# A fused linear-attention and gated-MLP kernel: the order of its steps searched anew under changed plan constants

## The chip, the core and the metric

The kernel runs on one core of one Trainium2 chip. The metric is the device time of one execution in microseconds (us), the median of several runs. The engines of the core are TensorE (PE in the profile, with its weight loads as PEld), VectorE (DVE), ScalarE (ACT), GpSimd (POOL) and SyncE (SP, which here only issues DMAs).

## What is computed

A quadratic-feature linear attention over 4 batches, 4 heads, 1088 positions and head dimension 32, followed by an RMS norm and a gated MLP (SiLU) over all 4352 positions with model width 128 and inner width 1536. All inputs are 32-bit floats.

```python
def phi(x):                       # 8 x 8 products = 64 features
    a = einsum('rd,bhsd->bhsr', S1, x)
    b = einsum('rd,bhsd->bhsr', S2, x)
    return einsum('bhsi,bhsj->bhsij', a, b).reshape(..., 64)
q_p, k_p = phi(q), phi(k)
kv  = einsum('bhsf,bhsd->bhfd', k_p, v)
num = einsum('bhsf,bhfd->bhsd', q_p, kv)
den = einsum('bhsf,bhf->bhs', q_p, sum(k_p over s)) + 1e-06
x   = (num / den) as [4352, 128]
xn  = x / sqrt(mean(x * x) + 1e-06) * rms_g
out = (silu(xn @ w_gate) * (xn @ w_val)) @ w_out
```

## The kernel before

The work falls into *steps* (the class Task). There are 1254 of them, numbered in the order in which the program adds them, and each carries the instructions of one piece of work on one engine:

- the key side of a batch (kside): loads of the keys kt and the values vt, the projection of the keys into PSUM (L519 for batch 0, L497 for the others), a copy both, the outer product phi, and the product with the values into kv (L531), which is copied into SBUF (steps 30 and 31 for batch 0, the tiles kv,0,0 and kv,0,1);
- the query side of a chunk (qside) of 512 positions (the ninth has 256): a load of q, its projection (L594 for chunks 0 and 1, L622 for the others), the outer product phiq, turned by PE for chunks 0 and 1 (L602) or spread through DRAM for the others (far, at, bt), the product with kv (L678), the division (den, rden, x), the squares ms, the inverse root rstd on POOL, the scaling xn, a transpose of xn (L758 for the first two chunks, through DRAM for the others) and the rounding into x_hi and x_lo;
- the weights: a load w_raw of 384 KB for each twelfth of the inner width, its head w_top, the joined w_full, the rounded w_hi and the remainder w_lo;
- the slots (slot): for each chunk c and each twelfth j three matmuls for the gate (g_ps, L802), three for the value (v_ps, L802), SiLU on ACT (s, L811), the product h on DVE (L814), its rounding h_hi and remainder h_lo (L832), and three matmuls into o_ps (L840). The three matmuls stand for one product of higher accuracy: high by high, low by high and high by low parts.

Nothing of the order is left to chance. The list ORDER gives the sequence of all 1254 steps, and the string ON gives, for the 354 steps that have a choice, the engine (a for ACT, d for DVE, p for POOL). Each engine works through its own steps in the sequence of the list, and the DMA issues of SP stand in the same list. The function follow walks along the list and works out, with constants for durations, semaphore hops, DMA flight and instruction fetches, when each step would start. Two things on the chip come of it: the sequence of emission (by planned start, which along one engine is the sequence in the list), and the fillers. Where the plan sees PE idle before EARLY (7 us), or idle for more than GAP behind it, it puts in matmuls on zeros that nobody reads (keep_warm, L382). The first seven of these stand there in any case.

Steps and lines that the argument follows: step 14 (g_ps from the first keys, L519) and step 18 (v_ps from the same piece of keys, L519); steps 32 and 37 (the two halves of query chunk 0, L594); step 428 (query chunk 3, L622, 16 matmuls); steps 56 and 61 (the transposes of the two halves of x of chunk 0, L758); step 66 (w_top of weight 0 on ACT, L401); steps 36 and 41 (phiq of chunk 0); steps 55 and 60 (the scaling xn of the two halves on ACT, L731), 57 (x_hi of the first half on ACT, L764); steps 186 and 190 (the first L802 matmuls of slot 1).

The starting parts of the plan's DMA model, the part of follow that the change touches:

```python
begin = max(wire, at + FLIGHT + OTHER * (w.since > 0))
wire = begin + w.lat
while fetches and fetches[0] < wire:
    wire += FETCH_WIRE * (begin < fetches.pop(0) + FETCH_WIRE)
t.end = wire + SETTLE + (w.occ - ISSUE if w.since else 0)
if len(landed) < len(LAGS):
    t.end += LAGS[len(landed)]
```

Of the kernel before, what the change touches and what calls it, by code (L numbers as in the profile page):

```python
# [39 lines left out]
LAGS = (210, 240, 740)  # L40
# [13 lines left out]
1 0 2 6 9 3 14 10 15 4 32 33 7 37 16 5 64 34 18 38 19 12 26 27 22 20 146 39 28 147 11 23 24 151 35 40 41 65 17 13 148 21 25 36 29 152 153 149 66 72  # L54
67 30 73 31 74 68 42 48 43 44 150 45 49 69 50 75 154 46 155 47 54 243 244 427 246 51 52 132 131 245 156 8 53 157 158 162 163 159 55 428 135 77 164
161 165 136 429 84 56 59 60 137 57 79 61 76 190 58 228 85 173 186 229 160 177 187 62 188 86 178 191 87 174 63 166 551 189 192 80 167 175 248 176 168
179 180 194 134 88 430 94 193 81 206 232 169 181 82 89 170 171 83 138 199 250 195 182 140 200 133 172 70 78 99 201 207 247 208 433 288 249 71 202 183
234 209 233 302 289 304 303 142 104 95 96 281 90 114 100 552 196 139 141 184 290 91 92 143 434 197 210 185 305 105 93 106 306 97 282 125 307 291 257
213 198 283 231 98 284 295 203 296 214 204 211 292 285 293 255 297 309 251 215 252 298 115 205 216 107 553 101 116 253 217 221 108 145 102 311 218
220 119 286 256 212 222 223 310 117 331 224 316 333 312 144 332 126 254 225 318 103 554 120 219 109 334 317 319 299 226 325 227 368 287 127 129 324  # L60
118 370 258 300 320 259 265 121 294 301 308 130 326 123 313 314 327 260 261 369 346 412 110 111 124 335 371 345 315 321 322 266 347 413 267 262 268
239 269 112 431 432 270 235 348 435 263 328 264 352 440 329 354 323 372 113 439 359 441 271 353 336 375 377 416 418 272 376 436 338 355 330 337 417
373 273 340 675 230 339 437 378 341 389 391 237 442 360 676 438 236 238 678 240 677 443 923 449 396 349 350 356 361 241 277 342 362 397 275 343 274
344 357 382 398 242 363 364 399 404 276 278 403 279 390 280 405 351 358 392 384 406 556 400 365 465 366 444 450 445 446 487 401 451 393 374 383 452
557 394 385 486 379 380 467 479 466 488 448 381 558 489 500 555 386 563 501 481 468 480 387 454 388 395 482 502 682 559 565 564 680 566 469 407 483
415 560 402 561 453 447 493 473 408 679 490 455 503 562 456 484 457 414 472 474 475 470 409 410 924 926 573 567 574 419 460 514 458 575 515 495 568
521 569 476 799 516 517 494 504 528 471 477 496 570 530 491 529 522 576 505 577 478 485 461 523 524 531 459 462 572 578 681 1047 684 497 411 542 532
535 498 544 463 537 492 533 571 518 579 536 525 499 538 507 464 508 589 509 590 526 510 511 591 592 580 519 603 543 605 581 512 545 604 596 624 606
506 513 520 527 534 925 598 626 685 689 625 546 582 610 539 421 540 597 627 688 585 541 547 683 686 617 593 584 612 611 607 608 583 586 587 599 631
619 613 594 618 548 645 549 633 687 690 632 800 802 801 804 620 420 929 422 697 423 691 424 639 600 601 805 614 634 635 636 659 660 661 662 595 588  # L70
692 602 647 646 806 621 638 693 615 609 698 648 652 699 654 426 653 616 628 640 622 649 629 650 425 666 655 727 641 623 729 656 694 642 803 643 721
728 730 668 720 722 657 700 630 702 667 755 695 723 713 715 637 928 813 812 696 811 701 814 669 809 670 644 651 663 671 703 704 714 930 757 734 664
756 550 758 807 658 748 665 735 716 724 808 810 705 717 709 736 784 1048 1049 725 737 750 738 731 128 707 718 739 1050 815 816 817 821 818 822 783
1052 672 742 741 673 706 708 785 732 786 759 743 719 726 760 749 733 744 710 776 823 777 1051 751 778 790 745 711 762 779 763 791 712 746 824 1053
752 792 793 769 740 764 753 927 936 837 747 931 826 771 754 780 765 770 839 761 825 367 766 767 820 893 794 935 838 819 827 795 844 772 840 894 933
773 781 768 895 1054 774 846 896 828 932 934 937 829 865 787 845 847 788 938 841 859 851 867 775 897 898 866 853 868 872 782 842 858 860 848 789 849
869 852 796 854 830 797 900 870 873 843 833 861 880 831 832 834 862 874 875 902 855 856 879 1059 881 1060 914 850 857 863 864 876 1061 882 901 1057
1055 886 1056 916 1062 945 883 939 884 1058 903 946 1063 887 798 947 888 877 948 835 674 836 1064 889 915 890 871 878 917 950 949 968 970 907 891 918
1065 909 908 885 989 910 969 971 961 963 940 941 942 919 904 943 962 911 964 944 951 905 892 899 991 1066 912 965 996 990 992 993 975 952 953 954 998
906 913 977 976 1067 1068 1069 1070 972 994 997 1003 920 978 982 973 983 999 966 921 984 979 980 1005 1004 957 967 1006 1010 1012 985 1038 1000 956  # L80
1040 974 122 1011 1013 1017 1024 986 1039 1001 1018 981 1026 1041 1042 1032 987 988 1007 1008 1019 1020 995 1002 955 958 959 1031 1043 960 1009 1033
1014 1034 1107 1129 1021 1071 1022 1073 1108 1109 1110 1015 1111 1079 1075 1128 1130 1131 1074 1081 1025 1027 1028 1016 1023 1029 1035 1036 1086 1088
1087 1093 1089 1094 1095 1096 1072 1076 1030 1077 1142 1097 1090 1091 1080 1082 1037 1044 1144 1045 1143 1101 1083 1100 1102 1084 1098 1085 1121 1145
1114 1116 1103 1104 1105 1146 1046 1078 1122 1092 1147 1123 1124 1115 1099 1135 1117 1118 1112 1149 1132 1137 1136 1106 922 1150 1133 1151 1172 1138
1152 1139 1113 1125 1174 1156 1119 1157 1179 1173 1158 1126 1165 1120 1127 1175 1140 1167 1153 1159 1154 1180 1181 1182 1134 1141 1160 1193 1187 1166
1161 1186 1168 1176 1195 1148 1200 1169 1188 1155 1177 1201 1189 1183 1184 1170 1194 1196 1214 1162 1202 1229 1203 1216 1197 1228 1163 1215 1207 1164
1190 1198 1230 1171 1178 1191 1185 1231 1243 1209 1217 1208 1218 1222 1245 1221 1232 1219 1210 1192 1199 1204 1205 1206 1223 1236 1233 1224 1211 1225
1212 1237 1226 1244 1213 1238 1246 1220 1227 1234 1240 1242 1247 1239 1249 1235 1251 1241 1253 1248 1250 1252
"""
ON = (  # L90
# [17 lines left out]
SWITCH = 138  # L108
RING, ISSUE, FAR, FLIGHT, SETTLE, RATE = 8, 470, 640, 900, 1300, 380
OTHER = 300  # L110
AHEAD, FETCHED, BLOCK, ASK, FETCH = 62, 210, 128, 2600, 2400
STALL = (3200, 0)
FETCH_WIRE, FETCH_AT = 1300, (9800, 16300, 26400, 31000)
COLD = (5600, 1.5)
# [35 lines left out]
class Plan:  # L150
# [32 lines left out]
    def follow(self, clock0, filler):  # L183
# [7 lines left out]
        for i in map(int, ORDER.split()):  # L191
            t = self.tasks[i]
            e = t.on
            w = t.ways[e]
# [757 lines left out]
```

## Time and profile before

| | us |
| --- | --- |
| median of three runs | 252.21 |
| lowest and highest run | 252.2, 252.3 |
| the profiled execution, time | 252.34 |
| the profiled execution, span from the first to the last instruction | 250.4 |
| PE busy in the span | 246.5 |
| DVE busy | 180.6 |
| ACT busy | 132.8 |
| POOL busy | 81.9 |

The profiled execution is one run of the program with the hardware profiler. Its span goes from the first instruction to the last; its time has some 2 us more around it. PE's instructions are pipelined, and their ends are modelled, so neighbouring rows overlap: the distance from start to start is the cost of one. The idle time in brackets behind a row is that of its engine just before it.

### The profile page before, as it was taken

What the parts mean: (1) busy time and instruction counts of PE and PEld (TensorE: products, weight loads), DVE (VectorE), ACT (ScalarE), POOL (GpSimd) and SP (SyncE); (2) the same over time, 40 slices, a digit from 0 to 9 for tenths busy, and PEclk for the clock granted to TensorE, in tenths of its full rate; (3) what the DMA queues carried; (4) which work ended last, traced back from release to release, by engine and by line L of the source; (5) the groups of instructions that cost most, each with busy time, mean ns of one, the idle gap of its engine ahead of it and who ended that gap; (6) DMA issues with size and microseconds to landing.
All of it is one profiled execution on the core that took longest, in us unless ns stands there. A gap on an engine that the chain in (4) does not pass through costs nothing.

```text
span 250.4 us, 5878 instructions
## 1 busy us (share of the span) xinstructions
PE 246.5 (98%) x2244; PEld 198.7 (79%) x2244; DVE 180.6 (72%) x410; ACT 132.8 (53%) x287; POOL 81.9 (33%) x80
## 2 busy tenths in 40 slices
PE   8999999999999999999999999999999999999995
PEld 5977788777888788878888788888888888888894
DVE  1899998789467887575587678855678576765672
ACT  3686988564444747353445643553356464355351
POOL 4447031343664223223550403265332203132201
PEclk9999999999999999999999999999999999999999
DMA  6989892552371332321610254251002102010010
GB/s 238 359 265 343 269 251 91 158 152 45 108 205 41 86 98 77 105 86 34 183 34 1 47 153 112 45 149 61 3 0 46 41 3 43 21 63 3 0 42 21
DMA packets 19691, 25.55 MB, mean 102 GB/s; under 512 B 3152, under 2 KB 11472, under 8 KB 19664
## 3 DMA queue, kind: packets, MB, share of 16 engines
q1 hardware_dynamic: 19232, 24.54, 33.3%
q10 hardware_dynamic: 432, 0.66, 0.7%
q8 instruction: 17, 0.28, 0.4%
q14 instruction: 10, 0.08, 0.1%
HBM read 20.40 MB, written 4.78 MB: 101 GB/s over the span
## 4 chain that ended last, share of the span: by engine, by line
PE 98%; DVE 0%; issue 0%
PE v_ps L802 29%; PE g_ps L802 29%; PE o_ps L840 28%; PE att L678 3%; PE att L531 2%; PE o_ps L382 2%; PE att L622 1%; PE o_ps L531 1%; PE att L594 1%; PE att L758 1%; PE att L497 1%; PE g_ps L678 0%; PE att L602 0%; PE v_ps L678 0%; PE att L821 0%; PE g_ps L519 0%
## 5 line engine op out<-in xcount | busy, mean ns | idle before, releaser
L811 ACT ACTIVATE s<-g_ps 128x512 f32<-128x512 f32 (+1 forms) x108 | 61.0, 574 | 71.4 <-PE g_ps L802 38.1
L814 DVE TENSOR_TENSOR h<-v_ps,s 128x512 f32<-128x512 f32 (+2 forms) x110 | 69.8, 647 | 40.0 <-PE v_ps L802 27.7
L832 POOL TENSOR_TENSOR h_lo<-h,h_hi 128x512 fp32r<-128x512 f32 (+1 forms) x42 | 52.9, 1267 | 104.5 <-DVE h_lo L832 43.9
L350 ACT CAST h_hi<-h 128x512 fp32r<-128x512 f32 (+1 forms) x70 | 41.3, 601 | 19.9 <-DVE h L814 17.4
L832 DVE TENSOR_TENSOR h_lo<-h,h_hi 128x512 fp32r<-128x512 f32 (+1 forms) x64 | 41.4, 652 | 5.5 <-ACT h_hi L350 3.6
L802 PE MATMUL v_ps<-x_hi,w_hi 128*128 128x512 f32 (+1 forms) x110 | 41.9, 381 | 0.0
L802 PE MATMUL g_ps<-x_hi,w_hi 128*128 128x512 f32 (+1 forms) x110 | 41.9, 381 | 0.0
L802 PE MATMUL v_ps<-x_hi,w_lo 128*128 128x512 f32 (+1 forms) x110 | 41.6, 378 | 0.0
L802 PE MATMUL g_ps<-x_hi,w_lo 128*128 128x512 f32 (+1 forms) x110 | 41.5, 378 | 0.0
L802 PE MATMUL g_ps<-x_lo,w_hi 128*128 128x512 f32 (+1 forms) x110 | 41.5, 379 | 0.0
L802 PE MATMUL v_ps<-x_lo,w_hi 128*128 128x512 f32 (+1 forms) x110 | 41.3, 378 | 0.0
L840 PE MATMUL o_ps<-h_hi,w_hi 128*128 128x512 f32 (+1 forms) x106 | 40.9, 386 | 0.0
L840 PE MATMUL o_ps<-h_hi,w_lo 128*128 128x512 f32 (+1 forms) x106 | 40.8, 385 | 0.0
L840 PE MATMUL o_ps<-h_lo,w_hi 128*128 128x512 f32 (+1 forms) x106 | 40.8, 385 | 0.0
L802 PEld LDWEIGHTS v_ps<-x_hi,w_hi 128*128 128x128 f32 x110 | 20.6, 188 | 5.0 <-DVE w_lo L436 0.5
L802 PEld LDWEIGHTS g_ps<-x_hi,w_hi 128*128 128x128 f32 x110 | 20.7, 188 | 4.6
L802 PEld LDWEIGHTS v_ps<-x_hi,w_lo 128*128 128x128 f32 x110 | 20.7, 188 | 4.3
L802 PEld LDWEIGHTS g_ps<-x_hi,w_lo 128*128 128x128 f32 x110 | 20.7, 188 | 4.3
L802 PEld LDWEIGHTS g_ps<-x_lo,w_hi 128*128 128x128 f32 x110 | 20.6, 188 | 4.2
L802 PEld LDWEIGHTS v_ps<-x_lo,w_hi 128*128 128x128 f32 x110 | 20.5, 188 | 4.1
L840 PEld LDWEIGHTS o_ps<-h_lo,w_hi 128*128 128x128 f32 x106 | 19.9, 188 | 4.4
L840 PEld LDWEIGHTS o_ps<-h_hi,w_hi 128*128 128x128 f32 x106 | 19.9, 188 | 4.2
(112 smaller groups left out, 246.9 us busy)
## 6 DMA issues: line engine op xcount, KB each, us to landing
w_raw<-w SPq DMA_DIRECT2D x12, 384.0 KB
bt<-far SPq DMA_DIRECT2D x24, 128.0 KB
at<-far SPq DMA_DIRECT2D x12, 256.0 KB
outT<-o_sb SPq DMA_DIRECT2D x16, 128.0 KB
q<-qT SPq DMA_DIRECT2D x7, 256.0 KB
turned<-xq SPq DMA_DIRECT2D x24, 64.0 KB
xt<-turned SPq DMA_DIRECT2D x6, 256.0 KB
vt<-v SPq DMA_DIRECT2D x4, 272.0 KB
```

The source lines that it names most:

```text
L350: "act": on_act(n, lambda: nc.scalar.copy(out=out(), in_=in_()), True),
L382: nc.tensor.matmul(out=warm[:1, :cols], lhsT=zeros[:, :1], rhs=zeros[:, :cols], start=True, stop=True)
L497: nc.tensor.matmul(out=pair[p]()[a * D:(a + 1) * D, :g], lhsT=sblk[p * HALF:(p + 1) * HALF, p * NB // 2:(p + 1) * NB // 2], rhs=kt()[p * H ...
L531: nc.tensor.matmul(out=kvv[r0:r0 + wide, h // 2, :], lhsT=phi()[:, t, h * F + f:h * F + f + wide], rhs=vt()[:, t, h, :], start=(t == 0 and ...
L594: nc.tensor.matmul(out=ab()[hf * HALF:(hf + 1) * HALF, t * HALF:(t + 1) * HALF], lhsT=q()[:, s1:s1 + HALF], rhs=sblk, start=True, stop=True,)
L622: nc.tensor.matmul(out=accs[p]()[a * D:(a + 1) * D, :m], lhsT=sab[rows, p].rearrange("p c o r -> p (c o r)"), rhs=q()[rows, a * m:(a + 1) ...
L678: nc.tensor.matmul(out=nv[n0:n0 + wide, t, p, :], lhsT=phi()[:, p, l0:l0 + wide], rhs=kvs[(s0 + l0) // S][:, p, :], start=True, stop=True,)
L802: nc.tensor.matmul(out=acc()[:, cs], lhsT=wt[:, j, i3, :], rhs=x()[:, cs], start=(i == 0), stop=(i == 2))
L811: act(n, lambda: nc.scalar.activation(out=s()[:, :n], in_=gps()[:, :n], func=AF.Silu), cols(gps, whole[0]), [s])
L814: cs.stop - cs.start, lambda cs=cs: nc.vector.tensor_tensor(out=h()[:, cs], in0=vps()[:, cs], in1=s()[:, cs], op=ALU.mult),
L832: eng.tensor_tensor(out=h_lo()[:, :n], in0=h()[:, :n], in1=h_hi().bitcast(F32)[:, :n], op=ALU.subtract)
L840: nc.tensor.matmul(out=o_ps()[:, :n], lhsT=wt[:, j, 2, :], rhs=x()[:, :n], start=first and i == 0, stop=last and i == 2,)
```

## The change

Five constants of the plan take other values (the lags of the first loads, ASK, FETCH, FETCH_WIRE and FETCH_AT), one is added (LATE, which the plan adds to the beginning of every load), and the list ORDER and the string ON are replaced by the outcome of a new search under these constants. No step is added, removed or altered. Of the lists the first two lines stand here.

```diff
@@ -37,7 +37,7 @@
 STEP, EARLY = 107, 7000
-LAGS = (210, 240, 740)
+LAGS = (120, 240, 700)
 NATURAL = 2
...
 ORDER = """
-1 0 2 6 9 3 14 10 15 4 32 33 7 37 16 5 64 34 18 38 19 12 26 27 22 20 146 39 28 147 11 23 24 151 35 40 41 65 17 13 148 21 25 36 29 152 153 149 66 72
-67 30 73 31 74 68 42 48 43 44 150 45 49 69 50 75 154 46 155 47 54 243 244 427 246 51 52 132 131 245 156 8 53 157 158 162 163 159 55 428 135 77 164
...
+0 6 1 2 3 14 15 18 19 16 20 9 10 7 32 64 37 33 38 22 34 26 27 151 28 39 146 13 11 23 8 147 35 152 40 41 12 65 72 24 148 153 66 67 5 73 243 131 17 21
+25 29 149 31 36 30 42 154 74 150 75 76 43 427 132 44 77 45 46 4 84 155 48 49 156 68 47 162 50 51 157 52 158 54 53 59 244 135 79 55 159 163 164 70 246
...
 """
 ON = (
-    "dapapadaddaadaadddaaaaapapdapapaadaadaadaapaadaadaadaadaddaadppddaapaadaaddadadadadadadadpdddaadddaaapapadadapapaadapapd"
...
+    "ddddpddapadadaadadaaaaapapddpapaadaadaapaadaadaapaadaadaadaappppaadpaadaaadadadadadddadapddddaaddadaadadadapapddaadaddda"
...
 )
@@ -108,9 +108,10 @@
 OTHER = 300
-AHEAD, FETCHED, BLOCK, ASK, FETCH = 62, 210, 128, 2600, 2400
+AHEAD, FETCHED, BLOCK, ASK, FETCH = 62, 210, 128, 3300, 2800
+LATE = 150
 STALL = (3200, 0)
-FETCH_WIRE, FETCH_AT = 1300, (9800, 16300, 26400, 31000)
+FETCH_WIRE, FETCH_AT = 1100, (9750, 15200, 24500, 32000)
@@ -234,7 +235,7 @@
             if e == "dma":
-                begin = max(wire, at + FLIGHT + OTHER * (w.since > 0))
+                begin = max(wire, at + FLIGHT + LATE + OTHER * (w.since > 0))
                 wire = begin + w.lat
```

Counted along both lists: 393 steps are on PE in both. ACT has 265 steps before and 261 after, DVE 375 and 381, POOL 66 and 64, and DMA 155 in both. 25 h_lo go from POOL to DVE and 18 from DVE to POOL; 22 h_hi go from DVE to ACT and 21 from ACT to DVE. Early in the list, on PE:

```
before 14 32 37 18 26 22 146 151 35 40 17 21 25 29 149 42 48 154 244 156 162 428 135 56 61 190 173 186 177 187 188
after  14 18 32 37 22 26 151 146 35 40 17 21 25 29 149 42 154 48 156 162 244 135 56 428 186 190 61 177 173 174 191
```

On ACT, before and after:

```
before 1 15 4 33 5 38 19 27 147 23 36 152 66 31 68 150 49 75 155 246 245 8 157 55 77 429 60 57 85 62
after  1 33 38 27 8 152 41 66 5 36 30 150 77 4 155 49 68 157 55 163 70 246 245 57 60 62 80 85 429 430
```

In the list of loads, before: the second, the first and the third piece of the values of batch 0 with w_raw of weight 0 ahead of the third; after: the third, the first, the second, then w_raw of weight 0.

## Rows read from the trace of the kernel before

**Rows 1.** The page: busy time by engine (part 1), the chain that ended last (4).

```profile
PE 246.5 (98%) x2244; PEld 198.7 (79%) x2244; DVE 180.6 (72%) x410; ACT 132.8 (53%) x287; POOL 81.9 (33%) x80
...
PE 98%; DVE 0%; issue 0%
```

**Rows 2.** Windows: stretch, length, busy (x) PE, PEld, DVE, ACT, POOL, clock, DMA, GB/s.

```profile
4.21:16.58 12.37, 12.22 (x280) 9.66 (x279) 9.96 (x33) 8.26 (x30) 6.07 (x7) 1.00 0.93 329
16.58:60.00 43.42, 43.42 (x437) 34.22 (x436) 38.61 (x85) 31.44 (x66) 15.38 (x13) 1.00 0.66 199
60.00:247.40 187.40, 187.40 (x1517) 152.93 (x1515) 131.21 (x291) 91.58 (x190) 58.01 (x47) 1.00 0.23 64
```

**Rows 3.** Timeline, PE: start us, us, line, operation, tiles, count [idle before].

```profile
4.62 0.27 PE L382 MATMUL o_ps<-const-float32-0.0 128*1 128x32 f32 x2
4.81 0.70 PE L594 MATMUL att<-sblk,q 128*64 128x64 f32 x8
5.44 0.46 PE L382 MATMUL o_ps<-const-float32-0.0 128*1 128x128 f32 x2
5.82 0.45 PE L594 MATMUL att<-sblk,q 128*64 128x64 f32 x8
6.10 0.75 PE L519 MATMUL v_ps<-sblk,kt 128*64 128x64 f32 x20
6.69 0.52 PE L519 MATMUL g_ps<-sblk,kt 128*64 128x64 f32 x12
...
14.58 0.45 PE L622 MATMUL att<-q,sab 64*32 64x128 f32 x16
14.82 0.42 PE L497 MATMUL g_ps<-kt,sblk 64*32 64x288 f32 x4
...
15.44 0.44 PE L758 MATMUL att<-ident,xn 128*128 128x128 f32 x2
15.81 0.38 PE L382 MATMUL att<-const-float32-0.0 128*1 128x128 f32 x2
16.34 0.41 PE L758 MATMUL att<-ident,xn 128*128 128x128 f32 x2 [0.15 <-PE att L382]
16.58 0.39 PE L802 MATMUL v_ps<-x_hi,w_hi 128*128 128x256 f32 x1
```

**Rows 4.** Tile h_lo: engine, operation, count: duration ns min/median/max, first and last start us.

```profile
L832 DVE TENSOR_TENSOR h_lo<-h,h_hi x64: 417/684/695, 26.8 to 243.8; 128x512 fp32r<-128x512 f32 x56, 128x256 fp32r<-128x256 f32 x8
L832 POOL TENSOR_TENSOR h_lo<-h,h_hi x42: 740/1292/1307, 33.6 to 244.5; 128x512 fp32r<-128x512 f32 x40, 128x256 fp32r<-128x256 f32 x2
```

**Rows 5.** Timeline, ACT (columns as in group 3).

```profile
8.30 0.59 ACT L344 COPY phiq<-g_ps 128x512 f32<-128x512 f32 x1
...
8.94 0.66 ACT L401 CAST w_top<-w_raw 128x384 f16<-128x384 bf16 x1
10.99 0.21 ACT L560 COPY kv<-att 64x66 f32<-64x66 f32 x1 [1.40 <-PE att L531]
...
13.70 0.44 ACT L344 COPY abt<-att 128x128 f32<-128x128 f32 x2
...
14.53 0.69 ACT L731 ACTIVATE xn<-x,rstd 128x128 f32<-128x128 f32 x2
15.12 0.28 ACT L350 CAST w_hi<-w_full 128x128 fp32r<-128x128 f32 x1
...
15.47 0.69 ACT L731 ACTIVATE xn<-x,rstd 128x128 f32<-128x128 f32 x2
16.07 0.46 ACT L764 ACTIVATE x_hi<-att,gain_t 128x256 fp32r<-128x256 f32 x1
```

**Rows 6.** Timeline, SP's issues of loads (columns as in group 3).

```profile
3.88 0.33 SPq L422 DMA_DIRECT2D w_raw<-w  x1
4.26 0.47 SPq L482 DMA_DIRECT2D vt<-v  x1
```

**Rows 7.** DMA queues from 9.9 to 11.3 us: packets, MB, share of 16 engines.

```profile
q8 instruction: 1, 0.02, 4.4%
```

## What the change will do to the time, told before the run

> **What bounds the kernel now.** I read the page first, then the chain of waits, then the busy time by stretch, then the timeline of TensorE and its neighbours in the first 17 us. The page says that TensorE (PE) is busy for 246.5 of 250.4 us and that the chain that ended last is PE for 98% [rows 1]: no other engine is on the path. The stretches say where the missing 2% lies. From the first L802 matmul at 16.58 us to the last matmul, PE is busy without a break: 43.42 of 43.42 us up to 60 us, then 187.40 of 187.40 us, at a granted clock of 1.00, which is the 2.4 GHz level [rows 2]. Before 16.58 us it is busy 12.22 of 12.37 us [rows 2], and that figure hides something: three small groups of L382 matmuls are fillers, which compute nothing and only keep the engine occupied [rows 3]. So the time is the sum of PE's own work, plus what PE waits or fills in the first 17 us, plus a tail of some 3 us behind the last matmul. What the reader is to see: a new order cannot shorten PE's work, so all that it can win lies in the holes of the head, and all that it can lose is a new hole anywhere.
>
> The largest possible win follows from the fillers. The hole between the first key matmuls and the first query matmuls runs from 4.62 to 4.81 (0.19 us). The next, before query half 1, runs from 5.44 to 5.82 (0.38 us). The third, between the two transposes of x, begins 0.44 us behind 15.44, at 15.88, when the first one is through, and runs to 16.34 (0.46 us) [rows 3]. Together 1.03 us, 0.4% of the time.
>
> **The change part by part.** *PE's work.* The numbers in ORDER name the same 1254 steps; counted along both lists, PE has 393 steps in each, with the same matmuls. What could differ is how often PE changes the shape in which its array is divided; counted along both lists there are 33 changes before and 33 after, of nearly the same pairs of shapes. Cost: 0.
>
> *Engines of the other steps.* ON moves 25 h_lo from POOL to DVE and 18 the other way, and swaps 22 against 21 h_hi between DVE and ACT. The rest (w_lo, phi, phiq) runs mostly the other way, nine to POOL and four to DVE. In all DVE has six steps more (381), POOL two fewer (64), ACT four fewer (261). One h_lo is 1.292 us on POOL and 0.684 us on DVE [rows 4], so six steps of that size are 4.1 us; DVE then has some 185 us of work against PE's 246 [rows 1]. Behind 60 us it is busy 131 of 187 us [rows 2]. The cover is PE's own queue of matmuls; if a late operand uses that up, each late us is one us of the end. I take 0, with the bound in the rivals.
>
> *The first two holes.* In the new order the step that makes v_ps from the first keys (number 18, twelve matmuls of L519) stands straight behind step 14. Both read only the first piece of the keys and sblk, so what step 14 has in hand serves 18 too, and 18 can run in the hole at 4.62. At its old place it takes 0.35 us: the 20 matmuls that begin at 6.10, of which twelve are its own, last 0.59 us until the next row at 6.69 [rows 3]. The two holes hold 0.57 us. If query half 1 still starts at 5.82, all of 18 has moved off the path: 0.35 us won. If that half is there sooner, up to 0.57 us. The plan now lets loads land 150 ns later while two of the three start-up lags are 90 and 40 ns shorter, so for this load, the third, it expects 110 ns more, and a filler may be made that much longer: 0.24 us at the lower end. I take 0.3 us, nearest to the unmoved 5.82.
>
> *Between 7 and 15 us.* The order of PE is almost kept (one swap of two steps), so the lead of 0.3 us lives on if its operands come. The gate is the pair of kv copies before the first L678. Before, one is on ACT at 10.99 [rows 5]. After, ACT first does phiq, w_top of weight 0, a sab copy and the other phiq, and then its kv copy. w_top was at 8.94 [rows 5], straight behind its neighbour, so its load had landed by then. That load now stands behind all three value loads, one of which (136 KB) was issued after it [rows 6]; at the 329 GB/s of this stretch [rows 2] 139 thousand bytes are 0.42 us. So w_raw is there at 9.4 at the latest; w_top 0.66, a sab copy of the length of kv's 0.21 and phiq 0.59 us [rows 5] bring ACT to 10.9, and kv's 0.21 us would put the gate at the old 11.2 us if the old 8.94 was already the landing. It was an upper bound: ACT was busy until then. I take the load as early enough, cost 0, and keep 0.3 us of loss (the whole lead) as the other end.
>
> *The third hole.* After, PE does the first transpose of x, then the query block of chunk 3 (step 428, 0.24 us from 14.58 to 14.82, previously ahead of the transpose [rows 3]) and then L802 at once; the second transpose comes behind four of these matmuls. 428 now fills the hole (0.24 us won), but the second transpose (0.24 us) has left it (0.24 us lost). On ACT, x_hi moves ahead of the second xn, 0.69 us, but den, a w_hi of 0.28 us and two abt copies of 0.44 us move ahead of x_hi. From the end of xn at 15.22 these 0.9 us less their overlaps lead to about 16.0, which is the old start of x_hi, 16.07 [rows 5]. So the first L802 stays 0.5 us behind x_hi, and the second transpose now waits for xn behind x_hi: 0.46 and 0.69 us against four matmuls of 0.12 us, about 0.1 us of new waiting. Net -0.1 us; the ends are -0.4 us (all of the 0.46 us hole left over again and no use of it) and +0.46 us (hole gone).
>
> *Fetches.* FETCH, ASK, FETCH_AT and FETCH_WIRE are constants of the plan; nothing on the chip is told by them. Between 9.9 and 11.3 us one block of instructions is fetched on queue q8 [rows 7], and PE has no idle time there: what it misses of 12.37 us [rows 2] is the 0.15 us in front of 16.34 [rows 3]. So a fetch cost PE nothing in the densest stretch of small matmuls. The Trainium skill, page "Runtime: NRT & Kernel Launch", section "Instruction fetch mechanics", says that the sequencer streams its instructions ahead by itself and that crossing a block is mostly hidden; by that rule the longer fetches in the plan answer to nothing on the chip, and the trace agrees. By the rule this part is 0, as in my sum; by the plan's own 2.8 us for one fetch it would be up to that much, once. What remains of it here is only that the search was steered by it.
>
> *Tail.* The two output halves change places; one copy of part, two additions and one store as before. 0.
>
> Sum: -0.3 + 0 + 0.1 + 0 = -0.2 us. The profiled execution has a span of 250.4 and a time of 252.34 us, 0.13 above the median 252.21; on the median the sum gives **252.0 us**, and the span would be 250.2.
>
> **The rivals.** *A, the holes close* (faster): the load of query half 1 is early and x_hi comes early, so at least half of 1.03 us goes. For it: 428 and 18 are both put into holes. Against: ACT's queue ahead of x_hi is no shorter. 252.2 - 0.7 = 251.5 us.
>
> *B, w_raw of weight 0 is late on ACT* (slower). ACT works in order; w_top stands there ahead of phiq and kv, without which no L678 can start. The two weight loads are queued next to each other, and DMA is saturated, 0.93 over the stretch [rows 2]. If weight 0 lands only with weight 1, one transfer later (384 KB at 329 GB/s, 1.2 us), ACT is late by 0.42 + 1.2 = 1.6 us at w_top. Of this 0.2 us of slack before the gate and the lead of 0.3 us are free; it decides from 0.5 us on, one to one, and costs up to 1.1 us: from 252.2 to 253.3, typically 252.9 us. For it: the load has moved back in the queue. Against: loads are served in order as far as the rows show.
>
> *C, nothing moves* within 0.1 us (252.2 us): the lead of 0.3 us is taken back at kv. It lies inside the forecast's own range, 251.75 to 252.65.
>
> **How the numbers follow.** Forecast with C 0.62, A 0.16, B or a like late operand in the first pass over the weights (DVE is busy 38.61 of 43.42 us up to 60 us [rows 2]) 0.22. A timing of this kernel can tell about 0.2% (0.5 us) from no change, so faster is below 251.7 and slower above 252.7. The range 251.4 to 253.0 leaves out some 0.04 below and 0.12 above. Faster 0.16, same 0.62, slower 0.22.
>
> **What would show it.** PE's busy time from the first L802 to the end stays unbroken, and the L382 group at 4.62 is gone or shorter; the key step runs there; L678 begins near 11.1 us instead of 11.44; the first L802 is at 16.0 to 16.6. Wrong would be: any idle row on PE behind 20 us, or a first L678 later than 11.5 (rival B), or an x_hi before 15.6 (rival A).

## The result, and the profile after

The changed kernel took 254.81 us (median of 6 runs, 254.22 to 256.53) against 252.25 us for the kernel before on the same chip; the ratio is 1.0113, with a 95% interval of 1.0078 to 1.0148. All ratios here are estimated from the single runs, leaving out one of after_again that lies over 1.5% above its fastest, so they are not the quotients of the medians. Slower was expected with a chance of 0.22, for a late load of a weight (rival B), and the time lies outside the range of 251.4 to 253.0 us. The profiled execution took 254.32 us, with a span of 252.5 us.

The page (busy time by engine, then the chain that ended last) and the waits of TensorE (PE: tile, line, releaser, us in total, times, longest). The changed kernel has one line more near its top, so L382 is now L383, L802 is L803, and so on:

```profile
PE 246.5 (98%) x2238; PEld 199.2 (79%) x2238; DVE 182.7 (72%) x416; ACT 132.7 (53%) x280; POOL 78.9 (31%) x78
...
PE 92%; DMA 3%; DVE 2%; issue 1%; ACT 1%; SPq 0%; DVEq 0%
...
PE att L532 <- issue: 1.7, 1, 1.7
PE att L595 <- DMA q<-qT: 0.3, 1, 0.3
```

PE is busy for the same 246.5 us as in [rows 1], so the additional time is idle time. The chain is no longer PE alone, and one wait has appeared with "issue" as its releaser: the engine waited for nothing that the profile knows as an operand. The windows say where it lies (stretch, length, busy (x) of PE, PEld, DVE, ACT and POOL, granted clock, DMA share, GB/s):

```profile
4.28:16.76 12.48, 11.96 (x272) 9.94 (x271) 10.02 (x34) 6.98 (x25) 6.18 (x7) 1.00 0.95 350
16.76:62.25 45.49, 45.49 (x563) 35.97 (x563) 41.19 (x89) 33.78 (x72) 14.81 (x14) 1.00 0.65 196
62.30:64.20 1.90, 0.20 (x23) 0.10 (x12) 1.07 (x3) 0.00 (x0) 0.62 (x1) 1.00 0.26 53
64.20:249.50 185.30, 185.29 (x1386) 151.22 (x1385) 129.59 (x288) 90.48 (x182) 54.78 (x44) 1.00 0.22 61
```

Where [rows 2] has no idle time behind the first L802, this trace has one hole, from 62.3 to 64.2 us; on both sides of it PE is as full as before. PE's timeline around it, and below it the same place before the change (start us, us, line, operation, tiles, count, [idle before]):

```profile
60.70 0.72 PE L498 MATMUL att<-kt,sblk 64*32 64x288 f32 x16
61.35 1.15 PE L532 MATMUL att<-vt,phi 128*32 128x34 f32 x111
64.21 0.46 PE L532 MATMUL att<-vt,phi 128*32 128x34 f32 x33 [1.71 <-issue]
64.49 1.16 PE L679 MATMUL att<-kv,phiq 128*32 128x66 f32 x64
```

```profile
60.76 0.45 PE L622 MATMUL att<-q,sab 64*32 64x128 f32 x16
61.14 1.44 PE L531 MATMUL att<-vt,phi 128*32 128x34 f32 x144
62.42 1.13 PE L678 MATMUL att<-kv,phiq 128*32 128x66 f32 x64
63.49 0.50 PE L802 MATMUL g_ps<-x_hi,w_hi 128*128 128x512 f32 x1
```

Both kernels run a burst of 224 small matmuls here, at nearly the same time. After the change it breaks off among the L532 matmuls, of which 111 of 144 have run, and the profile names no operand. What arrives meanwhile is a block of instructions. The queue of instruction fetches in short windows, after the change from 61.7 to 62.9 us and before it from 56.85 to 57.0 us (packets, MB, share of 16 engines):

```profile
q8 instruction: 1, 0.02, 4.9%
```

```profile
q8 instruction: 1, 0.02, 39.4%
```

The sixth transfer of this queue starts at 61.83 us after the change and at 56.89 us before it. PE ran dry: it started a matmul at 62.30 us and the next one at 64.21 us, 2.4 us after the transfer had started. So the forecast's zero for the fetches is the term that failed; the last matmul starts at 249.24 us instead of 247.17, 2.07 us later, of which 0.18 us were lost before the first L803 (16.76 against 16.58 us) and 1.9 us in the hole.

### The profile page after: what moved, and what is told of

The parts are those of the page before. It is cut to its first block, busy times and chain, and to the rows that moved or that the text cites. A ratio compares the mean times of both kernels' runs of the same rounds, so it can differ in the third digit from the quotient of the medians.

```text
span 252.5 us, 5878 instructions
## 1 busy us (share of the span) xinstructions
PE 246.5 (98%) x2238; PEld 199.2 (79%) x2238; DVE 182.7 (72%) x416; ACT 132.7 (53%) x280; POOL 78.9 (31%) x78
## 4 chain that ended last, share of the span: by engine, by line
PE 92%; DMA 3%; DVE 2%; issue 1%; ACT 1%; SPq 0%; DVEq 0%
PE g_ps L803 29%; PE v_ps L803 28%; PE o_ps L841 28%; PE att L679 3%; DMA w_raw<-w 2%; PE att L532 2%; DMA kt<-kT 1%; PE att L623 1%; PE att L498 1%; DVE w_full L397 0%; PE att L822 0%; DVE x L687 0%; PE att L759 0%; DVE sq L710 0%; ACT w_top L402 0%
## 5 line engine op out<-in xcount | busy, mean ns | idle before, releaser
L833 POOL TENSOR_TENSOR h_lo<-h,h_hi 128x512 fp32r<-128x512 f32 (+1 forms) x35 | 44.4, 1278 | 100.3 <-DVE h_lo L833 23.3
L833 DVE TENSOR_TENSOR h_lo<-h,h_hi 128x512 fp32r<-128x512 f32 (+1 forms) x71 | 45.6, 653 | 7.7 <-ACT h_hi L351 3.7
L803 PE MATMUL g_ps<-x_hi,w_hi 128*128 128x512 f32 (+1 forms) x110 | 42.2, 383 | 0.0
L803 PE MATMUL v_ps<-x_hi,w_hi 128*128 128x512 f32 (+1 forms) x110 | 41.7, 380 | 0.0
L803 PE MATMUL v_ps<-x_lo,w_hi 128*128 128x512 f32 (+1 forms) x110 | 41.6, 379 | 0.0
L803 PE MATMUL g_ps<-x_hi,w_lo 128*128 128x512 f32 (+1 forms) x110 | 41.5, 377 | 0.0
L803 PE MATMUL v_ps<-x_hi,w_lo 128*128 128x512 f32 (+1 forms) x110 | 41.4, 377 | 0.0
L803 PE MATMUL g_ps<-x_lo,w_hi 128*128 128x512 f32 (+1 forms) x110 | 41.4, 378 | 0.0
L803 PEld LDWEIGHTS g_ps<-x_hi,w_hi 128*128 128x128 f32 x110 | 20.6, 188 | 4.9 <-ACT x_hi L765 0.2
L803 PEld LDWEIGHTS v_ps<-x_lo,w_hi 128*128 128x128 f32 x110 | 20.6, 188 | 4.7 <-issue 0.5
L803 PEld LDWEIGHTS g_ps<-x_hi,w_lo 128*128 128x128 f32 x110 | 20.7, 188 | 4.4
L803 PEld LDWEIGHTS v_ps<-x_hi,w_hi 128*128 128x128 f32 x110 | 20.6, 188 | 4.3
L803 PEld LDWEIGHTS v_ps<-x_hi,w_lo 128*128 128x128 f32 x110 | 20.6, 188 | 4.3
L803 PEld LDWEIGHTS g_ps<-x_lo,w_hi 128*128 128x128 f32 x110 | 20.6, 188 | 4.2
```

The lines of the kernel that those rows point to most:

```text
L803: nc.tensor.matmul(out=acc()[:, cs], lhsT=wt[:, j, i3, :], rhs=x()[:, cs], start=(i == 0), stop=(i == 2))
L833: eng.tensor_tensor(out=h_lo()[:, :n], in0=h()[:, :n], in1=h_hi().bitcast(F32)[:, :n], op=ALU.subtract)
```

## The experiments

The theory: what decides is where the end of a block of instructions falls against the burst. The windows from the start to the burst count PE's matmuls, first before the change and then after it:

```profile
0.00:60.75 60.75, 59.83 (x731) 46.16 (x731) 49.81 (x121) 41.71 (x98) 24.01 (x34) 1.00 0.71 223
```

```profile
0.00:60.69 60.69, 59.40 (x725) 46.73 (x725) 50.24 (x122) 41.63 (x97) 23.46 (x34) 1.00 0.71 230
```

So the burst begins behind 731 matmuls before the change and behind 725 after it; PE runs dry behind 852 (725, 16 and 111). "Dry" means here that the last matmul before the hole has started. Rivals: the loads in flight at 60 us delay the transfer; or the new order itself stalls, wherever the blocks end. The table collects all runs: the number of matmuls ahead of the burst, the start of the sixth instruction transfer, the waits of PE with releaser "issue", the starts of the first L802 (L803) and the last matmul in the profiled execution, all in us, and the median with the ratio to the kernel before on the same chip.

```
kernel          burst at  transfer  waits     first L802  last    between  median  ratio [95%]
before          731       56.89     -         16.58       247.17  230.59   252.25
after           725       61.83     1.7       16.76       249.24  232.48   254.81  1.0113 [1.0078, 1.0148]
after_again     725       62.07     2.2       16.95       249.96  233.01   254.31  1.0050 [1.0011, 1.0089]
after_loads     725       61.81     2.0       16.71       249.45  232.74   256.14  1.0165 [1.0136, 1.0193]
after_shift14   739       56.34     -         16.94       247.62  230.68   252.22  0.9992 [0.9970, 1.0014]
after_shift6    731       58.05     -         17.28       248.00  230.72   252.22  0.9990 [0.9974, 1.0006]
after_early416  741       55.74     -         16.39       247.17  230.78   252.82  1.0011 [0.9999, 1.0023]
before_less6    725       60.56     0.3       16.67       247.93  231.26   253.10  1.0051 [1.0025, 1.0078]
before_shift42  773       51.29     2.2, 2.2  16.37       253.39  237.02   258.39  1.0230 [1.0202, 1.0259]
before_step18   727       59.87     0.7       16.36       247.54  231.18   253.44  1.0058 [1.0027, 1.0089]
before_step18b  731       56.72     -         16.37       247.04  230.67   252.36  0.9999 [0.9982, 1.0017]
mend            741       56.32     -         16.83       247.26  230.43   252.64  1.0016 [1.0003, 1.0029]
after_swap66    731       58.04     -         17.20       247.88  230.68   252.26  0.9983 [0.9960, 1.0007]
after_kvfirst   731       57.24     -         16.64       247.19  230.55   252.43  1.0003 [0.9991, 1.0016]
```

**The change once more.** No edit.

> The changed kernel once more, nothing altered. Theory F (fetch): the hole of 1.9 us on PE at 62.3 us is a wait for instructions; the block that PE needed was still being fetched (transfer on q8 from 61.83, PE goes on at 64.21). The wait comes back at the same matmul, the 853rd, and its length follows the start of that transfer, so times between 254 and 257 us. Theory O (operand): the hole is a late operand of the key product L532; it comes back with the same length, and the start of the q8 transfer does not matter.

The hole is there again, behind the same 852 matmuls, and 2.2 us long; the transfer starts 0.24 us later, is longer, and PE goes on 0.72 us later, as theory F has it and theory O does not. The runs reach from 251.74 to 255.38 us, and one is at 256.82. Three of the ten, 251.74 to 252.34 us, show no loss at all, below the times that theory F expected, so the stall is not the same in every execution.

**The loads taken away.** In ORDER four loads move away from 60 us:

```diff
-117 258 326 412 294 552
+117 258 326 412 230 231 294 552
...
-360 799 438 340 230 268
+360 438 340 268
...
-269 415 377 352 231 341
+269 377 352 341
...
-386 414 366
+386 414 415 366
...
-456 565 470
+456 565 799 470
```

> The changed kernel with four loads moved in SP's list, no step of another engine moved: the two value loads of batch 2 go from 50 and 52 us to 35 us, where SP stands idle, one value load of batch 3 from 51 to 66 us and the query load of chunk 6 from 50 to 74 us. The DMA queue is then all but empty at 55 us, where the fetch of the block that came late can be asked for. Theory L (the fetch was late because the loads were in flight): its transfer begins by 59 us instead of 61.8, there is no hole, time 252.2 to 252.7 us. Rival R (the start of that fetch has nothing to do with the loads): transfer near 61.8 us, hole of 1 to 2 us, time 254 us or more.

The DMA engines are empty ahead of the transfer (windows, columns as above), and it comes at 61.81 us all the same:

```profile
58.00:60.00 2.00, 2.00 (x10) 1.64 (x9) 2.00 (x4) 1.80 (x6) 0.67 (x1) 1.00 0.00 0
60.00:61.00 1.00, 1.00 (x20) 0.42 (x18) 1.00 (x3) 0.49 (x1) 0.00 (x0) 1.00 0.00 0
```

So other loads don't hold the transfer up, and this rival falls. The profile shows only the transfer and not the request for it; that the request is late is the likely reading.

**The blocks moved, the order kept.** The 7 fillers of 128 columns at the start become 14 of 64. The work is the same, and there are 14 matmuls more ahead of all others; every filler is 2 in the records:

```diff
-    for _ in range(WARM):
-        keep_warm(WARM_COLS * 4 // P)
+    for _ in range(14):
+        keep_warm(64 * 4 // P)
```

> The changed kernel with its seven filler matmuls of 128 columns at the start given as fourteen of 64 columns: the same columns, but fourteen more matmul records, so that every later matmul stands fourteen places further on in PE's instruction stream. Nothing else differs. Theory F: the block boundary then falls fourteen matmuls earlier in the work. The block is asked for some 3.3 us sooner (fourteen matmuls of 0.233 us) against the burst of 224 small matmuls, and 10.2 instead of 7.0 us lie between the place where it can be asked for and the place where PE runs dry. The hole goes, time 252.2 to 252.7 us. Theory O: no operand comes sooner; the hole of 1.9 us stays, 254.2 us or more.

In after_shift6 it is 4 fillers of 128 and 6 of 64, so that the burst begins behind 731 matmuls, as before the change:

> The changed kernel with three of its seven filler matmuls at the start given as six of half the columns: six more matmul records. In three looks at the changed order the transfer of the late block began at 61.8 to 62.1 us, 1.1 us behind the first matmul of step 416 (60.7 us), the head of the burst; with fourteen more records it began at 56.3. Theory H (the request lies in the instruction stream just behind the head of step 416, where PE's sequencer has to wait for the semaphore that PE itself gives at 60.08): six records move the request ahead of that head, so the transfer jumps to 57 to 59 us and there is no hole; 252.2 to 252.8 us. Theory G (the request follows the count of matmuls done, and simply takes long): the transfer moves by six matmuls of 0.233 us, to some 60.4 us, PE goes on 2.4 us later, and a hole of about 0.5 us is left.

Both take 252.22 us: 6 matmuls of no use at the start take the whole loss away, and the transfer comes at 56.34 us (14 matmuls) and 58.05 us (6). Theory O, with a hole in any case, falls, and so does theory G, with the transfer at 60.4 us and a hole of 0.5 us; theory H had 57 to 59 us. In after_shift6 PE is busy without a break through the burst:

```profile
61.30:64.30 3.00, 3.00 (x225) 2.39 (x224) 2.87 (x7) 0.62 (x1) 0.04 (x1) 1.00 0.39 79
```

**The old order on the new place.** The kernel before with 4 fillers of 224 columns for its 7 of 128, which takes 6 matmuls away (its tile of zeros is made 256 columns wide for that):

```diff
-    zeros = nc.const_aps.tensor(0.0, [P, P], F32)
+    zeros = nc.const_aps.tensor(0.0, [P, 2 * P], F32)
...
-    for _ in range(WARM):
-        keep_warm(WARM_COLS * 4 // P)
+    for _ in range(4):
+        keep_warm(224 * 4 // P)
```

> The kernel before, its order untouched, with the 7 fillers of 128 columns at the start made 4 of 224 (the same 896 columns, 6 matmul records fewer, so every later matmul stands 6 places nearer to the program's start, as in the changed kernel). If the stall behind 60 us belongs to where the blocks of the program fall against the burst of small matmuls, and to nothing in the new order, this kernel stalls too: the sixth instruction transfer near 60 to 62 instead of 56.9 us, a hole of 1 to 2.5 us with the releaser issue inside the burst, median 253.8 to 255. If it belongs to the new order: transfer at 57, no such hole, 252.3 to 252.5.

The transfer moves from 56.89 to 60.56 us and the wait appears in the old order, in the same step:

```profile
61.40 1.19 PE L531 MATMUL att<-vt,phi 128*32 128x34 f32 x115
62.88 0.42 PE L531 MATMUL att<-vt,phi 128*32 128x34 f32 x27 [0.30 <-issue]
```

The time is 253.1 us, below the 253.8 to 255 expected, with single runs of 255.06 to 255.84. The place alone makes the stall, in the old order too. Its size is smaller here, which fits the transfer: this one started 0.5 us ahead of the burst (61.02 us), the one after the change 1.1 us behind it (60.70 us).

**A shift by 42.** The kernel before with 28 fillers of 32 columns:

```diff
-    for _ in range(WARM):
-        keep_warm(WARM_COLS * 4 // P)
+    for _ in range(28):
+        keep_warm(32 * 4 // P)
```

> The kernel before, with its seven filler matmuls at the start given as 28 of 32 columns: the same columns, 42 more matmul records. By theory F two bursts of small matmuls, near 62 and 114 us, now leave only 1.6 us each between the place where the next block can be asked for and the place where PE runs dry; in the runs of before and after no fetch came within less than 3 us of that place. Two holes of 1.5 to 2 us each on PE, released by nothing but issue; time 255 to 256.5 us. Theory O, and any theory in which only the new order is at fault: no hole, 252.2 us.

Two holes, behind 983 and 1494 matmuls: 131 and 642 more than 852, which is one and five times 128, and 3 or 2 more. (In before_less6 PE ran dry behind 856.) Here the seventh transfer falls into the burst (62.95 us, with PE dry at 63.05). Its timeline behind the first hole shows a second price, and the windows the granted clock:

```profile
62.30 0.97 PE L678 MATMUL att<-kv,phiq 128*32 128x66 f32 x50
65.44 0.43 PE L678 MATMUL att<-kv,phiq 128*32 128x66 f32 x14 [2.17 <-issue]
...
67.27 0.63 PE L802 MATMUL v_ps<-x_hi,w_lo 128*128 128x512 f32 x1
67.69 0.63 PE L802 MATMUL v_ps<-x_lo,w_hi 128*128 128x512 f32 x1
...
66.00:68.00 2.00, 2.00 (x6) 1.59 (x6) 0.00 (x0) 0.92 (x2) 0.00 (x0) 0.58 0.14 32
68.00:70.00 2.00, 2.00 (x6) 1.54 (x6) 1.12 (x2) 0.80 (x2) 1.28 (x1) 0.57 0.65 227
70.00:72.00 2.00, 2.00 (x10) 1.61 (x9) 0.33 (x1) 0.15 (x1) 0.00 (x0) 1.00 0.66 186
```

From 66 to 70 us the mean granted clock is 0.58 and 0.57, most of it at the lower level of 1.2 GHz. Matmuls of 512 columns then follow each other every 0.43 us in place of 0.23 us; some seven of them cost about 1.5 us. The two holes (2.4 us each, from start to start) and this make up nearly all of the 6.4 us by which "between" has grown. The time, 258.39 us, lies above the 255 to 256.5 expected, which had no such price. The single runs agree with it: the three with a mean clock of 0.993 took 258.20 to 258.71 us, the one at 1.000 took 257.04 us.

**The burst cut.** In the changed kernel step 416 (16 matmuls of L498) runs six PE steps earlier:

```diff
-268 263 336
+268 416 263 336
...
-273 416 558
+273 558
```

> The changed kernel with one step moved: step 416 (the projection of the keys of batch 3, 16 matmuls) goes six PE steps forward, into the wide matmuls, as the order before has it. It costs two more changes of the array's shape, about 0.3 us. Theory H: the head at which the sequencer waited no longer stands in front of the request; the transfer begins by 59 us, no hole or one under 0.5 us; 252.5 to 253.0 us. Rival (the burst of small matmuls as such, whatever stands at its head): the burst still holds 208 small matmuls and the transfer still comes near 61.8 us; hole of 1.5 us, 254 us.

No stall; the transfer starts at 55.74 us, as the 16 small matmuls at 56.13 us are next. The main burst now begins behind 741 matmuls and is 208 long. This changes the place too, so it doesn't tell whether step 416 itself held the request up. The expected price of the array's shape is not there in full: the rows have one change more, not two, and "between" is 0.1 us above the versions without a hole at 230.68 us.

**Step 18 alone, without and with the old place.** The kernel before with step 18 behind step 14:

```diff
-3 14 10 15
+3 14 18 10 15
...
-34 18 38
+34 38
```

> The kernel before with one step moved: number 18 straight behind 14, as in the changed order, and the fillers that the plan then sets (one of 128 columns fewer or more). My step on the first two holes says 0.3 us less, 251.9 to 252.1 us. Rival: the lead is taken back at the kv copies or at x_hi, no change within 0.1 us.

The first L678 came at 10.95 us (11.44 before) and the first L802 at 16.36 us (16.58), yet the time rose to 253.44 us, outside both expectations. The plan had put in fewer fillers, the burst stood behind 727 matmuls, and PE waited 0.7 us for "issue". In before_step18b four matmuls are given back (5 fillers of 128 columns, 4 of 64):

> The kernel before with step 18 moved directly behind step 14, as before_step18, and with 4 records more at the start (7 fillers of 128 columns become 5 of 128 and 4 of 64), so that the number of matmul records ahead of 20 us is that of before again. If the 253.4 of before_step18 came from its 4 missing records: no hole with the releaser issue, the sixth transfer near 57 us, and the gain of the closed hole shows, 251.9 to 252.3. If moving step 18 itself costs: 253.0 or more, without such a hole.

252.36 us and no such wait. The 1.1 us between these two kernels come from 4 matmuls at the start. The first L802 is 0.2 us earlier in both than before, but whether step 18 does that isn't shown: with step 18 at its old place it came at 16.67 us in before_less6 and at 16.37 us in before_shift42. In the time nothing can be told from 0.

**What held the kv gate.** mend is the changed kernel with 14 fillers of 64 columns and, in the head, the loads and steps in an order nearer to the one before:

```diff
-64 37 33 38
+64 12 11 65 13 37 33 38
...
-146 13 11 23
+146 23
...
-40 41 12 65 72
+40 36 41 72
...
-67 5 73 243
+67 5 243
...
-29 149 31 36 30
+29 31 73 149 30
```

> The changed order with fourteen more filler records at the start and its loads of batch 0 as in the order before: the load of weight 0 ahead of the third value load instead of behind all three, phiq ahead of w_top on ACT, and the second kv copy ahead of w_top of weight 1 on DVE. Theory B (in the changed kernel w_top of weight 0 stood idle for its load until 9.91 us, and 10.09 us with the fourteen records, and held up both kv copies): the first L679 comes at 11.1 to 11.4 us instead of 11.90 and 12.07, and the time falls by 0.4 to 0.8 us against after_shift14, to 251.4 to 251.8 us. Rival: the first L802 is set by the chain on ACT and DVE behind L679 anyway, and the time stays at 252.2 us.

In after_swap66 and after_kvfirst, both with the fillers of after_shift6 and none that the plan adds behind the first matmuls, ACT does phiq (36) ahead of w_top of weight 0 (66):

```diff
-40 41 12
+40 41 36 12
...
-29 149 31 36 30
+29 149 31 30
```

> The changed kernel with 6 records more at the start (as after_shift6, 252.2) and, on ACT, phiq of unit 0 (step 36) ahead of w_top of weight 0 (step 66) and sab (step 5); the one filler that the plan then adds at 10.9 us is left out. If the wait of w_top for its load is what holds the kv gate: the first L679 moves from near 12 to 11.2 to 11.5 us and the time to 251.6 to 251.9. If the gate is held elsewhere (the q load, VectorE's kv): L679 stays at 11.9 to 12.4 and the time at 252.2.

In after_kvfirst VectorE also does kv (31) ahead of w_full (67) and w_top of weight 1 (73). Against after_swap66:

```diff
-153 66 67 5 73
+153 66 5
...
-29 149 31 30
+29 31 67 73 149 30
```

> after_swap66 with, on VectorE, the eviction kv of block 0 (step 31) ahead of w_full of weight 0 (step 67) and w_top of weight 1 (step 73); no filler of the plan's is put in. If VectorE's queue behind the late load of weight 0 is what holds the kv gate: kv at 11.1 and the first L679 at 11.2 to 11.4 us in place of 12.34. If the second score group is then all that the first L803 waits for, it comes at 16.1 to 16.3 in place of 17.20 and the time is 251.3 to 251.7. If the chain of the norm or the weight's planes (x_hi, w_hi) sets the first L803, the gate's gain stays in the head: L803 at 16.6 to 17.2, and 251.9 to 252.3.

With ACT's order mended the gate (the first L679) stayed at 12.34 us; with VectorE's it opened at 10.95 us. The profile puts the wait in after_swap66 down to ACT's phiq, which ended at 12.20 us, 0.01 us behind VectorE's kv; but in after_kvfirst the gate opened before that phiq had begun (11.05 us), so it was kv. VectorE in the changed kernel, and then in after_kvfirst (timeline):

```profile
10.63 0.56 DVE L397 SCALAR_TENSOR_TENSOR w_full<-w_raw,w_top 128x384 uint32<-128x384 uint32 x1 [0.75 <-ACT w_top L402]
11.11 0.39 DVE L405 CAST w_top<-w_raw 128x384 f16<-128x384 bf16 x1
11.52 0.23 DVE L557 COPY kv<-att 64x66 f32<-64x66 f32 x1
...
10.51 0.23 DVE L557 COPY kv<-att 64x66 f32<-64x66 f32 x1 [1.45 <-PE att L532]
10.77 0.56 DVE L397 SCALAR_TENSOR_TENSOR w_full<-w_raw,w_top 128x384 uint32<-128x384 uint32 x1
...
12.58 0.17 DVE L699 TENSOR_SCALAR den<-g_ps 128x8 f32<-128x8 f32 x1
```

The gain doesn't reach the end. From after_swap66 to after_kvfirst the gate opens 1.4 us earlier and the first L803 comes only 0.56 us earlier (17.20, 16.64); in the profiled executions the last matmul starts 0.7 us earlier, and the medians (252.26 and 252.43 us, on different chips) don't differ measurably. What sets the first L803 is the first den on VectorE. It stands behind w_full, w_top, w_full and w_hi whether kv goes ahead of them or not, so it moved only from 13.14 to 12.58 us, the same 0.56 us; and in all eight versions of the changed order but mend the first L803 comes 4.05 to 4.06 us behind this den. In mend the gate opens at 11.15 us and den is at 12.39 us, yet the first L803 is at 16.83, 4.44 us behind it, released by ACT:

```profile
16.83 0.38 PE L803 MATMUL g_ps<-x_hi,w_hi 128*128 128x256 f32 x1 [0.18 <-ACT x_hi L765]
```

This x_hi waits for the first transpose of x, which starts at 15.86 us, behind a filler that the plan has put in at 15.33 us; in the other eight the transpose follows xn by 0.6 us, here by 1.1 us. So the time of mend, 252.64 us, is not the 251.4 to 251.8 us expected. An earlier gate alone buys only what it moves den. No version beat the kernel before by more than can be measured: the lowest ratio is 0.9983 with an interval that includes 1.

## Why the prediction was wrong

*Fetches: 0. This is the step that failed.* It took one block, fetched between 9.9 and 11.3 us [rows 7], and went on from "no idle time there" to every other block. The stretch there was dense, but what counts is how long PE has from the start of a transfer until it is dry. The starts of the transfers at the stalled places and the restarts of PE lie 2.3 to 2.9 us apart (61.83 and 64.21, 62.07 and 64.93, 61.81 and 64.43, 62.95 and 65.44, 118.65 and 121.54, 60.56 and 62.88, 59.87 and 62.52); from the end of the transfer it is 1.2 to 1.6 us in all seven. From the start of the transfer to the last matmul that PE still had it is 0.1 to 1.8 us at these seven, and 2.6 us or more at the other 190 blocks of the fourteen traces from the third block on, which have no hole. (The first two blocks of a trace, counted the same way, go down to 1.6 us without a hole, so this bound isn't shown there.) At 60.70 us PE ran through 127 small matmuls, 725 to 852, in 1.6 us, and the transfer started only 1.1 us behind the head of that burst. With the burst six places later, behind 731 matmuls, it started over 3 us ahead of the head, and the block was there in time. The plan had the place for running dry nearly right, matmul 850 (its constants 210 and 5 times 128). But it lets the request go out at matmul 702 (62 and 5 times 128), which PE reached at 55.26 us, and the block be there 6.1 us later (ASK and FETCH, where no load stands in the way), at 61.4 us, ahead of the 62.30 us at which PE ran dry. In the trace PE went on 8.95 us after matmul 702. This would explain why the search took this order; no run shows it. The forecast had named any idle row on PE behind 20 us as a sign that it is wrong; that sign came.

The Trainium skill, page "Runtime: NRT & Kernel Launch", section "Instruction fetch mechanics", says that instructions come in blocks of 16 KiB, 256 instructions, and that crossing one is mostly hidden. On the blocks the traces agree: one transfer is 0.02 MB, each matmul has its weight load, x2238 of both, and the holes lie behind 852, 856, 983 and 1494 matmuls, multiples of 128 apart but for up to 4. On the hiding they agree for all blocks but one in the changed kernel; for that one the measured 1.9 us decide. "Mostly" was read as "here too"; the part named the plan's own 2.8 us for a block but gave it no room in the range, no rival and no chance.

*PE's work and the engine swaps: 0, right.* Without the 1.9 us of the hole, 230.6 us lie between the first L803 and the last matmul, as before (230.59). The versions of the changed order without a hole have 230.43 to 230.78 us. PE has no wait on another engine's result behind 17 us. (Between 7 and 15 us the lists differ by more than the one swap told: 48 and 154 change places too, and 244 goes behind 162. No wait of PE shows for it.)

*The first two holes: -0.3, wrong.* Step 18 runs in the hole at 4.55 us as told. But query half 1, supposed to hold its 5.82 us [rows 3], came at 6.14 us, and PE waited 0.29 us for its load. That took the gain away here. It isn't always so: in after_loads, with the same head, that half starts at 5.42 us, and still the gate opens at 11.85 us, since the load of weight 0 decides. In before_step18, where the loads kept their order, the half starts at 5.41 us and the first L678 is 0.49 us earlier; but in before_less6, with step 18 unmoved, the half starts at 5.39 us and the first L678 is 0.42 us earlier too. So a gain by step 18 isn't shown. The rows of the changed kernel on PE, and those on ACT for the next two terms:

```profile
4.55 0.85 PE L520 MATMUL v_ps<-sblk,kt 128*64 128x64 f32 x12
5.19 0.66 PE L595 MATMUL att<-sblk,q 128*64 128x64 f32 x8
6.14 0.52 PE L595 MATMUL att<-sblk,q 128*64 128x64 f32 x8 [0.29 <-DMA q<-qT]
...
9.91 0.63 ACT L402 CAST w_top<-w_raw 128x384 f16<-128x384 bf16 x1 [0.25 <-DMA w_raw<-w]
...
15.05 0.69 ACT L732 ACTIVATE xn<-x,rstd 128x128 f32<-128x128 f32 x2 [0.57 <-POOL rstd L722]
16.21 0.49 ACT L765 ACTIVATE x_hi<-att,gain_t 128x256 fp32r<-128x256 f32 x1
```

*The kv gate: 0, wrong.* It opened at 11.90 us, behind the 11.5 us named as the mark of rival B. B's cause was right: w_top of weight 0 is at 9.91 us, past the bound of 9.4 us reckoned from [rows 6], and waits for its load. Its place was not: the queue that passes the delay on is VectorE's (w_full and w_top ahead of kv), as the last two kernels show, and not only ACT's. The gate was 0.46 us late, and that went on one to one, as B had it: the first den on VectorE starts 0.53 us later than before (12.70 and 12.17 us), the first xn 0.52 us. It became 0.18 us at the first L803 by what the next term won.

*The third hole: 0.1 us of loss, wrong in its sign.* From the first L678 to the first L802 it took 5.14 us before and 4.86 us after. That is 0.28 us won, inside the bounds (0.4 lost, 0.46 won). It was won on ACT: x_hi, now ahead of the second xn, starts 1.16 us behind the first xn in place of 1.54 us [rows 5]. The forecast let den, w_hi and abt use up that gain, from 15.22 to about 16.0 us; from den to x_hi they take 0.56 us (15.65 to 16.21 us).

*Tail: 0, right.* From the start of the last matmul to the end of the span 3.3 us, before and after.

The head thus lost 0.18 us instead of winning 0.2 us; that alone would have been no change, as the most likely case said. The fetch brought the sign. The 0.22 for slower had been given for a late operand, which cost 0.46 us at the gate and decided nothing; it had no part for a fetch. That the median lies 0.5 us above the profiled execution fits before_shift42: two of the six runs, 256.53 and 256.02 us, have a mean granted clock of 0.993, the mean that before_shift42 shows with its stretch at the lower level; the other four, at 0.999 and 1.000, took 254.22 to 255.01 us. No trace of those two executions is there, so this is argued.

Still open is what holds the transfer back until near the head of the burst: at places 725 and 727 it started at 59.87 to 62.07 us, at 731 to 741 at 55.7 to 58.1 us. It goes with that head: in the three stalled traces of the new order it starts 1.13 to 1.18 us behind the first matmul of the burst, in the two of the old order 0.43 to 0.46 us ahead of it. Also open is whether the single runs of the kernel before at 254.1 to 255.2 us (5 of 93 in the four later batches), for which there is no trace, are the same stall; its burst is 4 matmuls from the place where it appears.

## What to carry to other kernels

When a change only reorders work, look at where the blocks of instructions end against the bursts of small matmuls, and compare the time in which PE runs through such a burst with the time that a block takes to come. A single number of a dense stretch doesn't show that all crossings are hidden: list the instruction transfers, and for each the time until PE would run dry. And before an order is judged by its time, move it by a few idle instructions; if the time changes by more than they last, the order was not what was measured.

## What was not expected of the hardware

Six matmuls more or fewer at the start of the program, of the same length in sum, move the time by 0.6 to 2.6 us: 253.10 against 252.46 us in the old order, 252.22 against 254.31 to 254.81 us in the new one. A hole of 2.4 us can cost 1.5 us more behind it through the granted clock, which was at its lower level from about 66.3 to 69.7 us; the hole of the same length at 119 us in the same trace had no such fall behind it, its windows to 132 us all being at 1.00.
